# Who makes the fourth pair's x, and which queue stores the last layer's quarters: two lines of a fused attention and two-layer feed-forward kernel

## Chip, cores and metric

The kernel runs on one core of a Trainium2 chip, as one launch. The metric is the device time of an execution in microseconds (us). Three executions of the kernel before gave 876.63, 877.24 and 878.43 us; the median is 877.24.

## What is computed

Four batches of 576 tokens, eight heads of 64, go through an attention with exponential features, and the 2304 resulting tokens of 512 numbers through two feed-forward blocks:

```python
def phi(x):
    proj = np.einsum('bhsd,df->bhsf', x, w_phi)          # 64 -> 128 features
    proj = proj - np.max(np.abs(proj), axis=-1, keepdims=True)
    return np.concatenate([np.exp(proj), np.exp(-proj)], axis=-1)
q_p, k_p = (phi(q), phi(k))
kv = np.einsum('bhsf,bhsd->bhfd', k_p, v)
z = np.sum(k_p, axis=2)
x = np.einsum('bhsf,bhfd->bhsd', q_p, kv) / (np.einsum('bhsf,bhf->bhs', q_p, z)[..., None] + 1e-06)
# x as 2304 x 512
x = np.maximum(np.maximum(x @ w1, x @ w2), x @ w3) @ w_out      # 512 -> 768 -> 512
h = x @ w_in                                                    # 512 -> 2048
g = np.maximum(h, 0.0) + alpha * np.minimum(h, 0.0)
out = g @ w_out2                                                # 2048 -> 512
```

## The kernel before

**Stages.** A *pair* is two heads of one batch; there are 16, four to a batch. For each pair `keys` and `queries` project, take exponentials, and form the numerators and denominators. At the end of `queries` the denominators `nd` are copied to a small tile `dc` by DMA (L388), inverted on VectorE (L390, L391), written to device memory `r_d` (L393), read back broadcast over the 64 rows of each head into `xr` (L400, four DMAs), multiplied with the numerators (L402), and split into a high and a low part `x` (hi: L64 on ScalarE or L405 on GpSimd; lo: L70). Of each pair there are two halves of 288 tokens. With four pairs of a batch done, `layer1` can run: a *unit* is three products `p` of w1, w2, w3 with the x of all four pairs; its result is taken from PSUM by ScalarE (`s`, L436) and VectorE (L437, L439), and stored as `h_d` (L441). Attention of later pairs and units of earlier batches share TensorE for the first 370 us. Then come the product with w_out (L675, in eight *chunks* of 288 tokens, whose results `yo` ScalarE copies out of PSUM at L679), the first product of the second block (L773) and the last one (L861), both in a form with seven products where a plain one has eight.

**Conversions.** All this is done in float32 made of two parts, and the weights come as float64. A list `todo` of steps converts them: a load `st` (L493, from SyncE's queue, three buffers), four operations per tile on ScalarE (L77, L80) and VectorE (L84, L86) that make a word `wt` (eight buffers), and then either a split into the parts that TensorE reads (`wo`, `wi`), or, for the last layer's *quarters*, sums of words (L514) that `park` stores to `q_d` (L527), 28 stores of 256 KB in all. A word's buffer is free when its store has landed. The steps of quarters 0 and 1 and of w_out run at about 320 to 370 us, those of quarters 2 and 3 at 445 to 500 us. The stores are read back from 564 us on.

**What sets the order.** Each engine works through its own list, in order; the list is made when the kernel is built, by a scheduler with its own estimates of durations, from the program's order and from priorities (`tc.high_priority`). So an instruction that waits holds all that stands behind it on its engine, and moving one line can reorder much. SyncE (SP) and GpSimd (POOL) issue DMAs from such lists too. Unlike SP, GpSimd also computes: in the kernel before it makes x for the pairs 0 to 2 (`e = G`), VectorE and ScalarE for all others.

Of the kernel before, what the change touches and what calls it, by code (L numbers as in the profile page):

```python
# [23 lines left out]
NPAIR = H // 2  # L24
# [23 lines left out]
def tile_kernel(ctx: ExitStack, tc: tile.TileContext, qT, kT, tails, v, w_phi, w1, w2, w3, w_out, w_in, w_out2, alpha, out):  # L48
# [11 lines left out]
    nc = tc.nc  # L60
    V, A, G = nc.vector, nc.scalar, nc.gpsimd

    def hi_act(dst, src):
        A.activation(dst, src, AF.Copy)  # L64
# [4 lines left out]
    def sub(eng, dst, src, hi):  # L69
        eng.tensor_tensor(dst, src, hi.bitcast(F32), op=ALU.subtract)  # L70
# [36 lines left out]
    q_d = dram.tile([4, 7, P, 512], F32, name="q_d")  # L107
# [11 lines left out]
    def at(shape, dtype, name, tag=None, bufs=1):  # L119
        pool = ap if (tag or name) in KEYS_ONLY else lp  # L120
        return pool.tile(shape, dtype, name=name, tag=tag or name, bufs=bufs)
# [34 lines left out]
    def i_of(pair):  # L156
        return pair[0] * NPAIR + pair[1]
# [177 lines left out]
    def queries(pair):  # L335
# [26 lines left out]
        for g, tiles, pp in chain(project_queries(pair), tail()):  # L362
# [8 lines left out]
            if plain_kv(pair):  # L371
                e = dst[0]
            else:
                e = at([P, 2, 2, 256], F32, tag="qe", bufs=2, name="qe")[:, :, :, :w]
# [20 lines left out]
        for c in range(2):  # L395
            cs = slice(c * CH, (c + 1) * CH)
            xr = raw_tile()
            for h in range(2):
                r = slice(h * D, (h + 1) * D)
                nc.gpsimd.dma_start(xr[r], rows[h : h + 1, cs].to_broadcast([D, CH]))  # L400
            e = G if i_of(pair) < NPAIR - 1 else V
            e.tensor_tensor(xr, nd[0][:, cs], xr, op=ALU.mult)  # L402
            xh, xl = x_tiles(c)
            if e is G:
                G.tensor_copy(xh, xr)  # L405
            else:
                hi_act(xh, xr)
            sub(e, xl, xr, xh)
            res.append((xh, xl))
        xs[pair[0]].append(res)  # L410

    def raw_tile():
        return xs_.tile([P, CH], F32, tag="xr", bufs=3, name="xr")

    def x_tiles(half):
        t = x_tile(half)
        return t[:, 0], t[:, 1]
# [35 lines left out]
    for i, pair in enumerate(pairs):  # L453
        if i + 1 < len(pairs):
            load_pair(pairs[i + 1])
        with tc.high_priority(offset=(0, SOON, NOW, NOW)[pair[0]]):
            if i == PLAIN - 1:
                hi_dve(wph, wraw)
                sub(V, wpl, wraw, wph)
            run(*([at_priority(LATER, queries(last))] if last else []), keys(pair))  # L460
            last = pair
        count = CONVERT_IN[i] if i < len(CONVERT_IN) else 0
        for j in range(count):
            for _ in range(min(count, 4) if j == 0 else int(j + 3 < count)):
                fetch(begun[pair])
            with tc.high_priority(offset=LAST if i < NPAIR - 1 else 0):
                n = sum(len(x) for x in w)
                run(split_w123(n // 3, n % 3))
        u0 = 3 * (i - NPAIR) - LAG
        for u in range(u0, u0 + 3):  # L470
            if u >= 0:
                c, f = (u % 2, u // 2) if u < 12 else (u // NF1 % 2, u % NF1)
                layer1(u // 12, c, f, xs[u // 12], w[f])
    ap_ctx.close()
    sp = ctx.enter_context(tc.tile_pool(reuse_waits="tile", name="sp", bufs=1, side="right"))
    with tc.high_priority(offset=NOW):
        run(queries(last))
# [46 lines left out]
        return [lambda k=k: split_out(k) for k in range(NF1)], [w_out[k] for k in range(NF1)]  # L524

    def park(p, i, x):
        nc.gpsimd.dma_start(q_d[p, i], x)  # L527

    def do_quarters(p):
        b = {}  # L530

        def get(q):
            b[q] = words()

        def one():
            get(0)
            b[4] = both(word(), b[1], b[0])
            park(p, 0, b[0])
            park(p, 4, b[4])

        def two():
            get(3)
            park(p, 2, b[3])
            b[5] = both(word(), b[3], b[4])
            park(p, 5, b[5])
            park(p, 6, both(b[1], b[3], b[1]))

        def three_():
            get(2)
            park(p, 1, b[2])  # L550
            park(p, 3, both(word(), b[5], b[2]))

        return [lambda: get(1), one, two, three_], [w_out2[p, q] for q in (1, 0, 3, 2)]
# [388 lines left out]
```

## Time and profile before

| | us |
|---|---|
| median of three executions | 877.24 |
| the profiled execution's own time | 878.6 |
| its span, first to last instruction | 876.8 |
| TensorE matmul busy in the span | 868.5 (99%) |
| VectorE / ScalarE / GpSimd busy | 637.3 / 514.5 / 158.4 |

TensorE's granted clock is 1.0, the 2.4 GHz level, in all 40 slices. The busy figure of TensorE counts a matmul until its modelled end; a short wait shows as a gap between starts that is wider than the usual one. So the profile is read here by starts: the rows of TensorE in order of time, then the engine that the late row waits for, then what held that engine.

### The profile page before, as it was taken

What the parts mean: (1) busy time and instruction counts of PE and PEld (TensorE: products, weight loads), DVE (VectorE), ACT (ScalarE), POOL (GpSimd) and SP (SyncE); (2) the same over time, 40 slices, a digit from 0 to 9 for tenths busy, and PEclk for the clock granted to TensorE, in tenths of its full rate; (3) what the DMA queues carried; (4) which work ended last, traced back from release to release, by engine and by line L of the source; (5) the groups of instructions that cost most, each with busy time, mean ns of one, the idle gap of its engine ahead of it and who ended that gap; (6) DMA issues with size and microseconds to landing.
All of it is one profiled execution on the core that took longest, in us unless ns stands there. A gap on an engine that the chain in (4) does not pass through costs nothing.

```text
span 876.8 us, 17441 instructions
## 1 busy us (share of the span) xinstructions
PE 868.5 (99%) x6631; PEld 854.9 (97%) x6631; DVE 637.3 (73%) x1196; ACT 514.5 (59%) x1055; POOL 158.4 (18%) x278
## 2 busy tenths in 40 slices
PE   9999999999999999999999999999999999999998
PEld 8888899999999999999999999999999999999998
DVE  5578878877888776683965754846478899988871
ACT  4666767777677765553853554646477763544440
POOL 0354222112322244211112301111111000000000
PEclk9999999999999999999999999999999999999999
DMA  6445653223332169661688863745348746433321
GB/s 234 140 157 161 180 154 113 76 86 85 88 89 70 36 215 349 212 208 35 195 266 309 314 230 134 225 182 189 123 136 265 268 158 202 150 125 121 120 74 49
DMA packets 70436, 142.99 MB, mean 163 GB/s; under 512 B 9152, under 2 KB 36176, under 8 KB 70352
## 3 DMA queue, kind: packets, MB, share of 16 engines
q1 hardware_dynamic: 53664, 92.95, 33.2%
q0 software_dynamic: 14816, 45.26, 15.0%
q10 hardware_dynamic: 1872, 3.67, 1.2%
q8 instruction: 52, 0.85, 0.4%
q14 instruction: 32, 0.26, 0.1%
HBM read 93.07 MB, written 46.34 MB: 159 GB/s over the span
## 4 chain that ended last, share of the span: by engine, by line
PE 82%; issue 8%; DMA 4%; ACT 3%; DVE 2%; POOL 1%; POOLq 0%; DVEq 0%; ACTq 0%
PE acc L861 20%; PE p L265 16%; PE sums L773 12%; PE pj L265 6%; PE pc L773 6%; PE pn L265 6%; PE kvp L293 4%; PE p L675 3%; PE kvp L306 3%; PE pb L773 3%; DMA st<-in_w_out 2%; PE pt L368 2%; DMA xr<-r_d 1%; DVE wt L86 1%; DMA st<-in_w_in 1%
## 5 line engine op out<-in xcount | busy, mean ns | idle before, releaser
L265 PE MATMUL p<-x,w123t 128*128 128x288 f32 x1728 | 251.4, 298 | 0.4 <-ACT s L436 0.4
L265 PEld LDWEIGHTS p<-x,w123t 128*128 128x128 f32 x1728 | 235.0, 188 | 2.3 <-ACT s L436 0.8
L773 PE MATMUL sums<-x,wi 128*128 128x288 f32 x768 | 107.7, 295 | 0.0
L861 PE MATMUL acc<-wq,o 128*128 128x256 f32 x864 | 105.5, 283 | 0.0
L861 PEld LDWEIGHTS acc<-wq,o 128*128 128x128 f32 x864 | 104.2, 189 | 0.0
L773 PEld LDWEIGHTS sums<-x,wi 128*128 128x128 f32 x768 | 104.0, 188 | 0.0
L861 PE MATMUL acc<-wq,x 128*128 128x256 f32 x648 | 78.1, 280 | 0.0
L675 PE MATMUL p<-x,wo 128*128 128x288 f32 x576 | 77.0, 296 | 0.6 <-ACT yo L679 0.6
L675 PEld LDWEIGHTS p<-x,wo 128*128 128x128 f32 x576 | 76.6, 188 | 0.9 <-ACT yo L679 0.8
L861 PEld LDWEIGHTS acc<-wq,x 128*128 128x128 f32 x648 | 77.0, 188 | 0.0
L792 DVE SCALAR_TENSOR_TENSOR g<-neg,al,g 128x576 f32<-128x576 f32 x64 | 50.3, 811 | 23.6 <-ACT neg L791 23.6
L212 DVE TENSOR_REDUCE mx<-pj 128x4 f32<-128x512 f32 (+1 forms) x80 | 50.1, 628 | 12.3 <-PE pj L265 12.2
L781 ACT ACTIVATE s<-sums 128x576 f32<-128x576 f32 x48 | 31.1, 647 | 42.0 <-PE sums L773 41.9
L77 ACT ACTIVATE wt<-st 128x512 f16<-128x512 bf16 x38 | 30.1, 799 | 42.5 <-DVE wt L514 14.0
L793 POOL DMA_DIRECT2D g_d<-g x32 | 22.9, 715 | 167.2 <-DVE g L792 165.4
L441 POOL DMA_DIRECT2D h_d<-ho x48 | 28.2, 587 | 137.8 <-DVE ho L439 116.3
L245 ACT ACTIVATE ke<-pj,mx 128x128 f32<-128x128 f32 x96 | 36.9, 384 | 14.7 <-DVE mx L212 14.5
L293 PEld LDWEIGHTS kvp<-v,ke 128*128 128x128 f32 x320 | 40.6, 191 | 4.7 <-ACT kvf L318 1.8
L293 PE MATMUL kvp<-v,ke 128*128 128x128 f32 x320 | 42.9, 278 | 1.6 <-ACT kvf L318 1.6
L791 ACT ACTIVATE neg<-g 128x576 f32<-128x576 f32 x64 | 40.2, 675 | 6.3 <-DVE g L823 5.9
L64 ACT ACTIVATE o<-wt 128x512 fp32r<-128x512 f32 x45 | 27.4, 627 | 24.7 <-PE acc L861 14.2
L400 POOL DMA_DIRECT2D xr<-r_d x64 | 34.1, 539 | 32.3 <-DMA r_d<-dc 21.6
(161 smaller groups left out, 1779.6 us busy)
## 6 DMA issues: line engine op xcount, KB each, us to landing
g_d<-g POOLq DMA_DIRECT2D x32, 576.0 KB, 3.6
a<-g_d SPq DMA_DIRECT2D x36, 512.0 KB, 4.3
st<-in_w_out SPq DMA_DIRECT2D x22, 512.0 KB, 5.8
wst<-in_w SPq DMA_DIRECT2D x18, 512.0 KB, 4.0
st<-in_w_in SPq DMA_DIRECT2D x16, 512.0 KB, 4.7
yr<-y_d SPq DMA_DIRECT2D x28, 288.0 KB, 3.9
v<-in_v SPq DMA_DIRECT2D x16, 480.0 KB, 4.4
q_d<-wt POOLq DMA_DIRECT2D x28, 256.0 KB, 5.3
```

Source lines behind the costliest of these rows:

```text
L77: order(A.activation(half[:, :, 1].bitcast(F16), lanes[:, :, 3].bitcast(BF16), AF.Copy))
L212: V.tensor_reduce(mx, pv, axis=AX.X, op=ALU.max, apply_absolute_value=True, negate=True)
L245: A.activation(ev[:, a, 0], pv[:, a], AF.Exp, bias=mx[:, a : a + 1])
L265: nc.tensor.matmul(dst, x, y, start=i == 0, stop=i == len(ops) - 1, **kw)
L293: nc.tensor.matmul(kvp[:, j * P : (j + 1) * P], e[:, c], rv[:, t, j // 2 : j // 2 + 2].rearrange("p a d -> p (a d)"), start=first, stop=t ...
L400: nc.gpsimd.dma_start(xr[r], rows[h : h + 1, cs].to_broadcast([D, CH]))
L675: nc.tensor.matmul(p2[m // 2][1][:, m % 2], x, y, start=k + n == 0, stop=k == NF1 - 1 and n == 2)
L773: nc.tensor.matmul(dst[:, j], a, b, start=start and n == 0, stop=n == len(ops) - 1, skip_group_check=True)
L781: A.activation(s, src, AF.Copy)
L791: A.activation(neg, gv[:, j], AF.Relu, scale=-1.0)
L792: V.scalar_tensor_tensor(gv[:, j], neg, al[:, f + j : f + j + 1], gv[:, j], op0=ALU.mult, op1=ALU.add)
L861: nc.tensor.matmul(acc[i], x, y, start=half == 0 and f == 0 and n == 0 and place[i][1] == 0, stop=half == 1 and f == 3 and n == 2, skip_gr ...
```

## The change

Two lines. `e` in `queries` becomes GpSimd for the pairs 0 to 3 instead of 0 to 2, so for the fourth pair L402, L405 (instead of L64) and L70 are GpSimd's, twice each. And `park` issues its store from SP's queue.

```diff
             for h in range(2):
                 r = slice(h * D, (h + 1) * D)
                 nc.gpsimd.dma_start(xr[r], rows[h : h + 1, cs].to_broadcast([D, CH]))
-            e = G if i_of(pair) < NPAIR - 1 else V
+            e = G if i_of(pair) < NPAIR else V
             e.tensor_tensor(xr, nd[0][:, cs], xr, op=ALU.mult)
             xh, xl = x_tiles(c)
             if e is G:
@@
     def park(p, i, x):
-        nc.gpsimd.dma_start(q_d[p, i], x)
+        nc.sync.dma_start(q_d[p, i], x)
```

The instruction lists differ from the fourth pair on, on every engine. Three places follow.

**At 82 to 92 us.** GpSimd before, from the four loads of the fourth pair's `xr` on:

```order
L400 DMA xr<-r_d 64x288 x4
L388 DMA dc<-nd 64x1x9 x2
L389 DMA nd<-nd 64x576
L441 DMA h_d<-ho 128x288
L393 DMA r_d<-dc 128x9
L400 DMA xr<-r_d 64x288 x4
```

And now, from the same four loads on:

```order
L400 DMA xr<-r_d 64x288 x4
L402 TENSOR_TENSOR xr<-nd,xr 128x288
L388 DMA dc<-nd 64x1x9
L405 CAST x<-xr 128x288
L402 TENSOR_TENSOR xr<-nd,xr 128x288
L70 TENSOR_TENSOR x<-xr,x 128x288
L405 CAST x<-xr 128x288
L388 DMA dc<-nd 64x1x9
L389 DMA nd<-nd 64x576
L70 TENSOR_TENSOR x<-xr,x 128x288
L393 DMA r_d<-dc 128x9
```

Six computing instructions stand between the `xr` loads and the next pair's `r_d` store; the second half's lo part is behind the next pair's `dc` and `nd` DMAs.

TensorE before at that time, from the third product of the first unit that reads the fourth pair's x (`p_803`, `p_816`, `p_829` are its three results):

```order
L265 MATMUL p_829<-x,w123t 128x288
L265 MATMUL p_803<-x,w123t 128x288 x2
L265 MATMUL p_816<-x,w123t 128x288 x2
L265 MATMUL p_829<-x,w123t 128x288 x2
L293 MATMUL kvp<-v,ke 128x128 x7
L265 MATMUL pj<-wph,xhk 128x256
```

And now, from inside the first of the moved groups on:

```order
L265 MATMUL pj<-wpl,xhk 128x256
L265 MATMUL pj<-wph,xlk 128x256
L265 MATMUL pj<-wph,xht 128x256
L265 MATMUL pj<-wpl,xht 128x256
L265 MATMUL pj<-wph,xlt 128x256
L368 MATMUL pt<-ident,pp 128x128 x4
L265 MATMUL p_803<-x,w123t 128x288 x2
L265 MATMUL p_816<-x,w123t 128x288 x2
L265 MATMUL p_829<-x,w123t 128x288 x2
L293 MATMUL kvp<-v,ke 128x128 x8
```

Nine projections `pj` and four transposes `pt`, which stood behind the `kvp` group, now stand between the unit's first three products with the fourth pair's x and its last six.

**At 350 to 374 us.** ScalarE before, from the copy `s_4473` of a unit to `s_4836`:

```order
L436 ACTIVATE s_4473<-p_4434 128x288
L77 ACTIVATE wt<-st 128x512
L80 ACTIVATE st<-st 128x512
L436 ACTIVATE s_4746<-p_4707 128x288
L64 ACTIVATE x<-xr 128x288
L64 ACTIVATE wo<-wt 128x512
L436 ACTIVATE s_4791<-p_4752 128x288
L64 ACTIVATE wo<-wt 128x512 x5
L64 ACTIVATE x<-xr 128x288
L77 ACTIVATE wt<-st 128x512
L80 ACTIVATE st<-st 128x512
L436 ACTIVATE s_4836<-p_4797 128x288
```

And now, from `s_4746` on:

```order
L436 ACTIVATE s_4746<-p_4707 128x288
L77 ACTIVATE wt<-st 128x512
L80 ACTIVATE st<-st 128x512
L77 ACTIVATE wt<-st 128x512
L80 ACTIVATE st<-st 128x512
L64 ACTIVATE x<-xr 128x288
L436 ACTIVATE s_4791<-p_4752 128x288
L64 ACTIVATE wo<-wt 128x512 x6
L77 ACTIVATE wt<-st 128x512
L64 ACTIVATE x<-xr 128x288
L80 ACTIVATE st<-st 128x512
L436 ACTIVATE s_4836<-p_4797 128x288
```

The unit copies keep their order; the conversions L77 and L80 come about one unit later against them, and all six `wo` behind `s_4791`.

**At 466 to 487 us.** ScalarE before, around the copies `yo` of the fourth chunk (`yo<-p_6192` and `yo<-p_6193`):

```order
L77 ACTIVATE wt<-st 128x512
L681 DMA y_d<-yo 128x576
L80 ACTIVATE st<-st 128x512
L64 ACTIVATE x<-hr 128x576 x2
L77 ACTIVATE wt<-st 128x512
L679 ACTIVATE yo<-p_6192 128x576
L80 ACTIVATE st<-st 128x512
L64 ACTIVATE x<-hr 128x576
L679 ACTIVATE yo<-p_6193 128x576
```

And now:

```order
L77 ACTIVATE wt<-st 128x512
L80 ACTIVATE st<-st 128x512
L64 ACTIVATE x<-hr 128x576
L679 ACTIVATE yo<-p_6192 128x576
L64 ACTIVATE x<-hr 128x576
L679 ACTIVATE yo<-p_6193 128x576
L77 ACTIVATE wt<-st 128x512
L683 DMA y_d<-yo 128x576
L80 ACTIVATE st<-st 128x512
```

The second conversion has gone from ahead of both copies to behind both.

## Rows read from the trace of the kernel before

**Rows 1.** The page, busy us of each engine (share of the span) and instructions

```profile
PE 868.5 (99%) x6631; PEld 854.9 (97%) x6631; DVE 637.3 (73%) x1196; ACT 514.5 (59%) x1055; POOL 158.4 (18%) x278
```

**Rows 2.** The chain that ended last, in order of time: start us, us, what

```profile
373.85 34.13 PE p L265 x255
```

**Rows 3.** Timeline of PE from 86 us: start, us, instruction, [idle before <-releaser]

```profile
87.28 1.59 PE L265 MATMUL p<-x,w123t 128*128 128x288 f32 x9
90.45 1.83 PE L293 MATMUL kvp<-v,ke 128*128 128x128 f32 x14 [1.57 <-ACT kvf L318]
```

**Rows 4.** Timeline of ACT, 86 to 91 us

```profile
86.35 0.44 ACT L64 ACTIVATE x<-xr 128x288 fp32r<-128x288 f32 x1 [1.56 <-DVE xr L402]
...
87.91 0.45 ACT L64 ACTIVATE x<-xr 128x288 fp32r<-128x288 f32 x1
...
89.74 0.66 ACT L318 ACTIVATE kvf<-kvp 128x512 f32<-128x512 f32 x1
```

**Rows 5.** Timeline of DVE, 85 to 90 us

```profile
85.86 0.46 DVE L402 TENSOR_TENSOR xr<-nd,xr 128x288 f32<-128x288 f32 x1 [1.73 <-DMA xr<-r_d]
86.23 0.68 DVE L212 TENSOR_REDUCE mx<-pj 128x4 f32<-128x512 f32 x1
...
88.70 0.68 DVE L70 TENSOR_TENSOR xlq<-q,xhq 128x512 fp32r<-128x512 f32 x1
89.30 0.45 DVE L84 TENSOR_SCALAR wt<-wst 128x512 uint16<-128x512 uint16 x1
```

**Rows 6.** Timeline of POOL, 70 to 73 us: GpSimd makes the third pair's x

```profile
70.08 0.43 POOL L405 CAST x<-xr 128x288 fp32r<-128x288 f32 x1
70.47 0.80 POOL L402 TENSOR_TENSOR xr<-nd,xr 128x288 f32<-128x288 f32 x1
71.23 0.80 POOL L70 TENSOR_TENSOR x<-xr,x 128x288 fp32r<-128x288 f32 x1
71.99 0.66 POOL L405 CAST x<-xr 128x288 fp32r<-128x288 f32 x1
```

**Rows 7.** Timeline of DVE beside it

```profile
69.97 2.40 DVE L84 TENSOR_SCALAR wt<-wst 128x512 uint16<-128x512 uint16 x1
```

**Rows 8.** Timeline of PE around 355, 373 and 487 us

```profile
354.33 5.47 PE L265 MATMUL p<-x,w123t 128*128 128x288 f32 x36
...
371.27 2.18 PE L265 MATMUL p<-x,w123t 128*128 128x288 f32 x15
373.85 0.92 PE L265 MATMUL p<-x,w123t 128*128 128x288 f32 x5 [0.40 <-ACT s L436]
...
483.73 2.68 PE L675 MATMUL p<-x,wo 128*128 128x288 f32 x18
487.02 1.20 PE L675 MATMUL p<-x,wo 128*128 128x288 f32 x7 [0.61 <-ACT yo L679]
```

**Rows 9.** Timeline of ACT around 350 to 374 us

```profile
350.45 0.80 ACT L77 ACTIVATE wt<-st 128x512 f16<-128x512 bf16 x1 [3.42 <-DMA h_d<-ho]
...
367.91 0.45 ACT L64 ACTIVATE x<-xr 128x288 fp32r<-128x288 f32 x1 [5.14 <-DVE xr L402]
...
369.07 2.70 ACT L64 ACTIVATE wo<-wt 128x512 fp32r<-128x512 f32 x5
...
373.40 0.40 ACT L436 ACTIVATE s<-p 128x288 f32<-128x288 f32 x1
```

**Rows 10.** Timeline of ACT at 484 us, and of POOL ahead of it

```profile
479.50 0.54 POOL L527 DMA_DIRECT2D q_d<-wt  x1 [0.18 <-issue]
...
484.01 0.80 ACT L77 ACTIVATE wt<-st 128x512 f16<-128x512 bf16 x1 [5.11 <-issue]
...
486.33 0.64 ACT L679 ACTIVATE yo<-p 128x576 f32<-128x576 f32 x1
```

**Rows 11.** Waits: engine, line <- releaser: total us, times, longest; last row q_d's landing

```profile
SPq L603 <- DVE x L70: 33.8, 14, 7.9
...
DMA to landing us min/median/max: 2.7/5.2/7.9
```

## The prediction

> **What bounds the kernel now.** I read the busy line of the page first: TensorE is busy for 868.5 of 876.8 us, VectorE for 637.3, ScalarE for 514.5, GpSimd for 158.4 [rows 1]. So the bound is TensorE, and its clock stays at the upper level throughout. The change leaves the set of matmuls alone. It can move the end only through the places where TensorE's stream has a hole. To find the holes I took the length of a full stream from the chain of waits: 255 products of 128x288 in 34.13 us, 0.134 us each [rows 2]. Then I walked TensorE's timeline by starts, and wherever the next group begins later than count times 0.134 there is a hole.
>
> Up to about 82 us the instruction lists of both kernels are alike, so the start is the same in both. Behind that I find four holes:
>
> - At 87.28 nine products begin. They should end at 87.28 + 9 x 0.134 = 88.49, and the switch to the next kind of matmul costs some 0.2 (my estimate). The next row, `kvp`, begins at 90.45 and waited for ScalarE's `kvf` [rows 3]: a hole of 1.77.
> - At 354.33, 36 products take 5.47 where 4.82 are due [rows 8]. The modelled tail of the last one is some 0.1, so the hole is 0.54.
> - At 371.27, 15 products (2.01) should reach 373.28; the next begins at 373.85, after ScalarE's `s` [rows 8]: 0.57.
> - At 483.73, 18 products (2.41) should reach 486.14; the next begins at 487.02, after ScalarE's `yo` [rows 8]: 0.88.
>
> All four end on ScalarE, so the next view is its timeline. At 86.35 it had waited 1.56 us for VectorE's `xr`, and it then made two casts of x (0.44 and 0.45) in front of the exponentials, so that `kvf` came only at 89.74 [rows 4]. At 350.45 a conversion L77 had waited 3.42, at 367.91 a cast of x had waited 5.14 for `xr`, and behind that five `wo` copies (2.70) stood ahead of `s` at 373.40 [rows 9]. At 484.01 a conversion had waited 5.11 behind a store that GpSimd issued at 479.50, and the second `yo` came at 486.33 [rows 10].
>
> **Part 1: GpSimd makes the fourth pair's x.** Removed are two casts on ScalarE (0.9) and four operations on VectorE (two of L402 at 0.46, two of L70 at 0.45, [rows 5]); six operations on GpSimd are added. ScalarE loses the wait of 1.56 and the casts, so `kvf` comes at some 88.3 to 88.9, before TensorE can get to `kvp`, which now stands behind more work. The hole of 1.77 goes. Two things are late next.
>
> First, x itself. `xr` landed when VectorE began at 85.86 [rows 5]. On GpSimd the multiplication takes 0.80 and the cast 0.43 to 0.66 [rows 6]; between them now stands a DMA to `dc`, at the 0.54 of another issue on GpSimd [rows 10]. That gives 85.86 + 0.80 + 0.54 + 0.43 to 0.66 = 87.6 to 87.9, where TensorE arrives at 87.28 [rows 3]: a hole of 0.35 to 0.58. I take 0.5.
>
> Second, the moved projections. TensorE now does three products, six projections of 256 columns (by columns 0.134 x 256/288 = 0.12 each), and then `pj` with `xht`, which needs the buffer that VectorE's `pp` (L216) empties. It arrives there at about 87.8 + 3 x 0.134 + 6 x 0.12 = 88.9. On VectorE `pp` stands behind the `mx` that ended its wait, `xlq` (0.68) and the conversion L84 (0.45) [rows 5]. With the x work gone, L84 comes up for execution from 87.3 on, just when GpSimd is at the cast. What happens then is in one row: at 69.97, beside the third pair's x on GpSimd, the same L84 took 2.40 instead of 0.45 [rows 7], until after the cast (70.08), the multiplication (70.47) and the subtraction (71.23 to 72.03) [rows 6]. It was held for 2.40 - 0.45 = 1.95. In the changed kernel cast, multiplication and subtraction last from 87.2 to about 89.4. So L84 ends near 89.6, and `pp`, a 128x512 operation like the 0.68 ones [rows 5], at about 90.2. Less 88.9 that is a hole of 1.1 to 1.3. I take 1.1; it is zero if `pp` gets in first.
>
> The sum here is 0.5 + 1.1 - 1.77 = **-0.2**. The ends are -1.5 (x at its early time, `pp` not held) and +0.6 (TensorE waits for the whole x chain, and L84 is held once more for half a microsecond). The lo half of the second x stands behind the next pair's DMAs and is ready near 92, where the products that read it come some microseconds later; I cost it at nothing. If that cover went, it would be one multiplication, 0.80 [rows 6].
>
> Here a rule speaks against the change. The row shows L84 held for 1.95 us, through three operations of GpSimd [rows 6, 7]. The Trainium skill, "SBUF — State Buffer", section "Who interferes with whom", says that VectorE and GpSimd share one pair of ports, that whichever begins first keeps it for its whole instruction, and that the other is blocked meanwhile. The trace agrees that there is blocking, but by that rule L84 would have waited for one GpSimd instruction. I go by the row for the sum; the other reading is a rival below.
>
> **Part 2: the last layer's stores go to SP.** The issue itself (0.54 each, [rows 10]) leaves GpSimd, which is not the bound. What matters is when a store goes out, since a word's buffer is free only when its store has landed, 2.7 to 7.9 us later, 5.2 in the middle [rows 11], and ScalarE's L77 waits for that with unit copies or `yo` queued behind it. Together with the altered order:
>
> - 350 to 374 us. The conversions stand about one unit later against the unit copies, the six `wo` all behind `s_4791`, and the last pairs' inversion L390 and L391 stands some four conversions earlier on VectorE. Each of the two holes is shorter than what it loses from in front of it (0.54 against a wait of 3.42; 0.57 against five `wo` of 2.70, [rows 8, 9]). I take both as gone: **-1.1**. The ends are -1.1 and 0.
> - 485 us. The L77 that had waited until 484.01 now stands behind both `yo`. The second `yo` then starts when its products are done. **-0.9**; the ends are -0.9 and 0.
> - SP works in order. A store there stands behind loads that themselves wait. The nearest rows are SP's waits at L603, 33.8 us in 14 waits, 2.4 in the mean, 7.9 the longest [rows 11]. Most stores come right behind a load `st` that waits for the same VectorE operation, so I take nothing for this; the other end is a rival.
>
> **The sum.** -0.2 - 1.1 - 0.9 = -2.2. Against the profiled execution's 878.6 that gives 876.4. That execution lies 1.4 above the median of 877.24, so on the median the forecast is **875.0**. What this kernel's measurement can tell from no change is about 0.2%, 1.75 us.
>
> **The rivals.**
>
> *The hold on L84 is short.* If L84 is blocked for one GpSimd instruction only, it waits 0.6 for the cast, `pp` ends near 88.9, and TensorE has no second hole there. The first place is then worth 0.5 - 1.77 = -1.3, the whole -3.3: 873.9. For it speaks that a hold depends on which of the two begins first; against it that [rows 7] shows the long one at the same pair of operations. The rule on the shared ports gives this case.
>
> *The holes at 354, 373 and 487 only move.* TensorE's results must be taken by ScalarE, whose work is not less there: the same conversions stand a little later, and the next copy may find them in front of it. Then only the first place remains: -0.2, 877.0. For it speaks that ScalarE waits come from landings of stores [rows 9, 11], which stay as long; against it that L77 and the `yo` have changed places outright.
>
> *Slower: a store stuck on SP.* A store of quarters 2 and 3 stands behind a load L603 whose buffer is not yet free; the word's buffer comes free later, an L77 on ScalarE waits, and a `yo` behind it holds TensorE. The hole at 487 shows that `yo` there has no slack [rows 8]. With a hold between the mean and the longest of SP's waits, (2.4 + 7.9)/2 = 5.2 [rows 11], the time is -2.2 + 5.2 = +3.0: 880.2. It comes out slower than the kernel before from a hold of 2.2, and measurably so from 4.0. Against it: on GpSimd the store stood in a queue that works in order too, and eight words give room.
>
> *The change does nothing.* The lists exclude that: all engines' orders differ at the places named.
>
> **How the numbers follow.** The forecast has a chance of 0.44, of which 0.12 falls short of 1.75 us because a part of one gain is missing; the short hold 0.10; the holes that only move 0.28, of which 0.02 comes out slower by a new hole; the stuck store 0.18, 0.02 of it too small to measure. Faster: 0.32 + 0.10 = 0.42. Same: 0.12 + 0.26 + 0.02 = 0.40. Slower: 0.02 + 0.16 = 0.18. The lower end of the range takes every best end, -1.5 - 1.1 - 0.9 = -3.5, and the 0.6 by which the fastest run lies below the median: 873.1. The upper end takes the first place at +0.6 with no gain elsewhere, 877.8, and the 1.2 by which the slowest run lies above the median: 879.0. Beyond it lies most of the stuck store, some 0.17.
>
> **What would show it.** Right, if after the change `kvp` follows without a wait for `kvf`; TensorE waits about 0.5 for GpSimd's x near 87.3 and about 1.1 for VectorE's `pp` near 89, with an L84 of over 2 us beside GpSimd's cast; there is no hole before the products at 373 and 487; and GpSimd has no rows of L527. An L84 of 0.45 to 1.1 there would show the short hold. New waits of TensorE for `s` or `yo` at neighbouring units would show that holes only moved; a wait on SP ahead of a store, with a long L77 and a late `yo` behind, the stuck store. The forecast is wrong if either shows up with more than half a microsecond, or if a hole opens where none of these places is.

## The result, and the profile after

The changed kernel takes 883.86 us (median of 8 executions, 881.55 to 889.21) against 877.84 for the kernel before (8 executions, 876.09 to 881.20). The ratio is 1.0073, 95% interval 1.0048 to 1.0098: slower by 0.7%, where 875.0 had been forecast, and beyond the upper end of the range, 879.0. The profiled execution has a span of 882.3 us, 5.5 more than that of the kernel before. (One execution of an experiment below, 995.8 us, ran at a mean granted clock of 0.798; it is left out of every comparison, and that kernel was run a second time.)

TensorE's work is the same set of matmuls in both kernels. So the two traces can be laid side by side by count: wherever the first n matmuls, in order of their starts, are the same set in both, the difference between the starts of the next one is what the changed kernel has lost by then. This table is worked out in that way:

| matmuls issued | before, at us | after, at us | after is late by |
|---|---|---|---|
| 362 | 61.20 | 61.48 | 0.28 |
| 578 | 94.64 | 94.75 | 0.11 |
| 661 | 105.91 | 106.37 | 0.46 |
| 808 | 125.69 | 130.54 | 4.85 |
| 2405 | 330.91 | 336.51 | 5.60 |
| 2719 | 373.85 | 380.28 | 6.43 |
| 3560 | 485.59 | 491.68 | 6.09 |
| 3565 | 487.02 | 492.35 | 5.33 |
| last | 873.05 | 878.27 | 5.23 |

In this pair of traces the place at 82 to 92 us gained 0.2, as forecast, and the place at 487 us gained 0.8. At 331 to 374 us, where 1.1 was to be gained, 0.8 was lost, and another 0.8 between 126 and 331 us. But most of the loss, 4.4 us, arose between 106 and 126 us, at a place of which the prediction doesn't speak. (A second trace of the changed kernel, from one of the experiments, loses 4.35 between the same two counts.) TensorE after, in order of time (start, us, instruction, idle before and its releaser; what answers to [rows 3], and the new place):

```profile
87.54 0.80 PE L265 MATMUL p<-x,w123t 128*128 128x288 f32 x3
88.72 0.39 PE L265 MATMUL pj<-wph,xhk 128*128 128x256 f32 x1 [0.38 <-ACT ke L246]
...
90.44 0.36 PE L265 MATMUL pj<-wph,xht 128*128 128x256 f32 x1 [0.76 <-DVE pp L216]
...
116.97 1.01 PE L265 MATMUL p<-x,w123t 128*128 128x288 f32 x5
120.43 0.49 PE L293 MATMUL kvp<-v,ke 128*128 128x128 f32 x2 [2.45 <-ACT ke L245]
120.67 3.05 PE L265 MATMUL p<-x,w123t 128*128 128x288 f32 x12
123.52 0.41 PE L265 MATMUL pj<-wph,xht 128*128 128x256 f32 x1
```

At 120.43 TensorE had stood still for 2.45 us. And the twelve products behind it took 123.52 - 120.67 = 2.85 us, where twelve take 1.61 at the upper level [rows 2]. The granted clock by stretches (window in us, its length, PE busy and count, clock, DMA share, GB/s) tells why:

```profile
119.00:120.00 1.00, 0.00 (x0) 1.00 0.00 0
120.00:121.00 1.00, 0.57 (x4) 0.94 0.00 0
121.00:122.00 1.00, 1.00 (x6) 0.50 0.20 14
...
123.00:124.00 1.00, 1.00 (x7) 0.50 0.87 111
124.00:125.00 1.00, 1.00 (x9) 0.85 0.41 96
```

From about 121 to 124.3 us it is 0.50, the 1.2 GHz level, right behind the time in which TensorE did nothing. That costs half of some 3.4 us: 1.7. Hole and clock together are 4.2 of the 4.4 us.

Who was late is read on the other engines. ScalarE, VectorE and GpSimd after, in this order, each by its timeline:

```profile
110.90 0.45 ACT L357 ACTIVATE nd<-pn 128x320 f32<-128x320 f32 x1
...
120.01 0.37 ACT L245 ACTIVATE ke<-pj,mx 128x128 f32<-128x128 f32 x1 [5.61 <-DVE mx L212]
```

```profile
117.94 0.17 DVE L390 TENSOR_SCALAR dc<-dc 128x9 f32<-128x9 f32 x1 [3.68 <-DMA dc<-nd]
...
118.69 1.28 DVE L212 TENSOR_REDUCE mx<-pj 128x4 f32<-128x512 f32 x2
```

```profile
112.61 0.54 POOL L388 DMA_DIRECT2D dc<-nd  x1 [1.75 <-ACT q L377]
```

Read backwards: `kvp` waits for an exponential `ke` of the eighth pair's keys, that for the maximum `mx`, and `mx` stood on VectorE behind L390, the first step of the inversion of the sixth pair's denominators. L390 waited 3.68 us for the DMA that brings them, which GpSimd had issued at 112.61; and that stood behind the copy `nd` on ScalarE at 110.90. TensorE had finished the projections that `mx` reads by 111.9. The same copy, L390, `mx`, `ke` and `kvp` in the kernel before (rows of its ScalarE, of its VectorE, and of ScalarE and TensorE):

```profile
107.98 0.44 ACT L357 ACTIVATE nd<-pn 128x320 f32<-128x320 f32 x1 [0.61 <-PE pn L265]
```

```profile
114.04 0.17 DVE L390 TENSOR_SCALAR dc<-dc 128x9 f32<-128x9 f32 x1 [3.03 <-DMA dc<-nd]
...
118.68 0.68 DVE L212 TENSOR_REDUCE mx<-pj 128x4 f32<-128x512 f32 x1
```

```profile
119.94 0.37 ACT L245 ACTIVATE ke<-pj,mx 128x128 f32<-128x128 f32 x1
120.64 0.38 PE L293 MATMUL kvp<-v,ke 128*128 128x128 f32 x2
```

Two things differ. The copy is 2.9 us later after the change, since in ScalarE's list it now stands behind seven more exponentials, a cast of a weight and a conversion; L390 gets its data 3.9 us later. And TensorE's list asks for the product earlier: in the kernel before 767 matmuls stand ahead of it, now 740. TensorE arrives at 118.0, where in the kernel before it had other products to do until 120.64. There VectorE waited 3.03 for the same DMA, and no matmul was late for it. The margin was small even so: the exponential `ke` that this `kvp` reads ended at 119.94 + 0.37 = 120.31, 0.33 before the product began.

### The profile page after: what moved, and what is told of

Its sections match the earlier page's. It is cut to its first block, busy times and chain, and to the rows that moved or that the text cites. A ratio compares the mean times of both kernels' runs of the same rounds, so it can differ in the third digit from the quotient of the medians.

```text
span 882.3 us, 17422 instructions
## 1 busy us (share of the span) xinstructions
PE 871.5 (99%) x6631; PEld 857.2 (97%) x6631; DVE 639.6 (72%) x1192; ACT 514.9 (58%) x1053; POOL 147.6 (17%) x256
## 4 chain that ended last, share of the span: by engine, by line
PE 78%; DMA 4%; DVE 2%; issue 1%; ACT 1%; POOL 0%; DVEq 0%; ACTq 0%
PE acc L861 20%; PE p L265 18%; PE sums L773 12%; PE p L675 9%; PE pc L773 6%; PE pn L265 3%; PE kvp L306 3%; PE pj L265 3%; PE pb L773 3%; DMA st<-in_w_out 1%; DMA xr<-r_d 1%; PE pt L368 1%; DMA st<-in_w_in 1%; DMA r_d<-dc 1%; PE kvt L325 0%
## 5 line engine op out<-in xcount | busy, mean ns | idle before, releaser
L77 ACT ACTIVATE wt<-st 128x512 f16<-128x512 bf16 x38 | 30.0, 797 | 39.3 <-DMA st<-in_w_out 11.0
L293 PEld LDWEIGHTS kvp<-v,ke 128*128 128x128 f32 x320 | 40.2, 191 | 5.2 <-ACT ke L245 3.2
L293 PE MATMUL kvp<-v,ke 128*128 128x128 f32 x320 | 42.4, 278 | 2.8 <-ACT ke L245 2.7
L64 ACT ACTIVATE o<-wt 128x512 fp32r<-128x512 f32 x45 | 27.4, 627 | 25.1 <-PE acc L861 13.4
```

The source lines that it names most:

```text
L77: order(A.activation(half[:, :, 1].bitcast(F16), lanes[:, :, 3].bitcast(BF16), AF.Copy))
L293: nc.tensor.matmul(kvp[:, j * P : (j + 1) * P], e[:, c], rv[:, t, j // 2 : j // 2 + 2].rearrange("p a d -> p (a d)"), start=first, stop=t ...
```

## The experiments

Each was compared with the kernel before on the same chip, whose median lay between 877.1 and 878.0. An edit moves the lines behind it, so in the rows of some experiments L390 is L393 or L411, and L293 is L296, L297 or L302.

**One line at a time.** First only x on GpSimd, then only the stores on SP: each is the changed kernel with the other line of the diff as it was before.

> The first line alone: GpSimd makes the fourth pair's x, the stores stay on GpSimd. All engines' lists equal those of the changed kernel up to about 320 us. Theory (the whole loss lies at 104 to 132 us, in the order that the first line brings: a hole of 2.5 us ahead of kvp at 120 us, 1.7 us at the lower clock behind it, and two small holes): the same loss there, so about 6 us above the kernel before, and a granted clock of 0.998 to 0.999 in most runs; behind 320 us the row of the kernel before (0.57 at 373, 0.9 at 487), so 883 to 885. Rival (the stores on SP bring the loss, by filling the DMA engines or by holding ScalarE): 877 or below.

> The second line alone: the stores of the quarters go out from SP, x as in the kernel before. All lists equal those of the kernel before up to about 320 us. Theory: no hole at 120 us, clock 1.000, the 0.9 at 487 us goes, and 355 to 373 us stays within half a microsecond of the kernel before; so 0.4 to 1.4 below it, 876.5 to 877.5. Rival (the stores on SP bring the loss): 4 to 6 above it.

The first line alone gives 885.10 (ratio 1.0095, 1.0081 to 1.0109). Its trace has the hole ahead of `kvp` at 120.60, 2.0 long, and by the count of matmuls it is 4.1 late at 808: the loss is that of the first line. It also has holes at 350 to 362 us that come to 2.4. Whether the stores cost more from GpSimd than from SP in this order can't be told: the intervals of this kernel and of the changed one overlap. The second line alone came out at 878.94 (1.0028, 1.0013 to 1.0043), against the expectation of a gain. It was run again:

> The second line alone, once more, for a profile at the upper clock. The run before gave 879.0 against 877.1, 1.9 above the kernel before, where 0.4 to 1.4 below had been expected. Theory now (the gain of 0.9 at 487 us is there, but at 340 to 380 us new waits come that cost more): holes of 2 to 3.5 us in all at 340 to 380 us, none before, none at 487; 878 to 880. Rival (the difference is noise between runs): 876 to 877.5.

881.33 (1.0039, 1.0022 to 1.0055): slower again, so the second line is no gain either when it stands alone. There is no hole at 487 us; a new one is at 342. TensorE and VectorE of this kernel, and its windows:

```profile
342.40 3.77 PE L265 MATMUL p<-x,w123t 128*128 128x288 f32 x15 [2.19 <-DVE ho L439]
```

```profile
338.65 0.48 DVE L84 TENSOR_SCALAR wt<-st 128x512 uint16<-128x512 uint16 x1 [0.74 <-DMA st<-in_w_out]
340.91 0.46 DVE L402 TENSOR_TENSOR xr<-nd,xr 128x288 f32<-128x288 f32 x1 [1.79 <-DMA xr<-r_d]
...
341.89 0.45 DVE L439 TENSOR_TENSOR ho<-p,s 128x288 f32<-128x288 f32 x1
```

```profile
338.00:340.00 2.00, 2.00 (x17) 1.00 1.05 405
...
341.00:342.00 1.00, 0.00 (x0) 1.00 1.05 402
...
343.00:344.00 1.00, 1.00 (x6) 0.50 1.49 184
```

VectorE waits in its list for the DMA that brings `xr`, and `ho`, which frees TensorE's bank, stands behind that. The same two rows of VectorE in the kernel before:

```profile
337.62 0.44 DVE L439 TENSOR_TENSOR ho<-p,s 128x288 f32<-128x288 f32 x1
...
344.05 0.45 DVE L402 TENSOR_TENSOR xr<-nd,xr 128x288 f32<-128x288 f32 x1
```

There `ho` stands ahead of the multiplication that needs `xr`, and no matmul is late. So this hole is made as the one at 120 us is: a new order has put short work for TensorE behind a wait for a DMA. Again the clock goes to 0.50 behind it. The DMA engines are full (shares of 1.0, 400 GB/s), but they are as full in the kernel before (a share of 1.02, 400 GB/s at 340 to 345 us), and the transfers are only somewhat slower: at 328 to 350 us the median landing is 7.8 us for the stores (6.1 in the kernel before) and 7.1 for `xr` (6.5). How much of the hole that adds was not tried. It is not the hold that the rival in the prediction had: SP's waits at L603 are shorter than before (10.8 us in 10 waits, against [rows 11]).

**Pinning the late copy.** An order edge without a wait puts one row of ScalarE's list ahead of others; the other lists are then made anew too, TensorE's from its 678th matmul on:

```diff
+                pin = i_of(pair) == 7 and g == 0 and a > 0
+                with tc.issue_after(copied[5].ins) if pin else nullcontext():
                     A.activation(ev[:, a, 0], pv[:, a], AF.Exp, bias=mx[:, a : a + 1])
                     A.activation(ev[:, a, 1], pv[:, a], AF.Exp, bias=my[:, a : a + 1], scale=-1.0)
...
-                A.activation(nd[h][:, o : o + w], pn[:, :w], AF.Copy)
+                copied[i_of(pair)] = A.activation(nd[h][:, o : o + w], pn[:, :w], AF.Copy)
```

> The changed kernel, with one thing pinned on ScalarE: the copy of the sixth pair's second half of denominators (nd) stands ahead of six exponentials of the eighth pair's keys, as it does in the kernel before, not behind them. Theory (this copy is 2.9 us late; the inversion of the denominators on VectorE waits 3.7 us for it through a DMA, with the maximum mx and so the exponential behind it that kvp on TensorE waits for): the hole of 2.5 at 120 us and the lower clock behind it go, 4.2 us together, so 879 to 880.5. Rival (kvp is late because VectorE and ScalarE have too much to do there, whatever waits): the hole stays, 883 to 885.

880.41 (1.0036, 1.0023 to 1.0048), the time that the theory gave, with the clock at 1.000 in all five executions. But its trace doesn't show what the theory said. TensorE's waits there:

```profile
108.24 0.49 PE L296 MATMUL kvp<-v,ke 128*128 128x128 f32 x2 [1.64 <-ACT ke L247]
...
122.01 0.49 PE L296 MATMUL kvp<-v,ke 128*128 128x128 f32 x2 [0.32 <-ACT ke L247]
```

```profile
117.89 0.17 DVE L393 TENSOR_SCALAR dc<-dc 128x9 f32<-128x9 f32 x1 [1.40 <-DMA dc<-nd]
```

ScalarE had waited 3.02 us for an `xr` just ahead, and the copy came at 112.76, later than the 110.90 of the changed kernel; L390 ran at 117.89, as there. The hole of 1.64 lies ahead of the point where TensorE's lists differ, behind that late `xr`; the second trace of the changed kernel has one of 1.41 there too. What differs is when the second `kvp` is asked for: 756 matmuls stand ahead of it in place of 740, TensorE comes to it at 121.70 in place of 117.98, and 0.32 of the wait is left. The clock didn't fall. Between 661 and 808 matmuls this kernel loses 1.0 us against the kernel before, where the changed kernel loses 4.4. A further 1.8 was gained at 335 to 377 us, where the lists differ too. So a late L390 does no harm when TensorE asks for `kvp` late enough. That an earlier copy would help isn't shown by this run.

**Moving one product.** The `kvp` product that waits is put behind the next twelve products `p`; nothing else changes in any list:

```diff
+                    pin = i_of(pair) == 7 and t == 2
+                    with tc.issue_after(ready[0, 1, 1, 0].ins) if pin else nullcontext():
                         nc.tensor.matmul(
                             kvp[:, j * P : (j + 1) * P],
...
-            products(p[:, :CH], ops)
+            ready[b, c, f, j] = products(p[:, :CH], ops)
```

> The changed kernel, with a single matmul moved: the kvp product for which TensorE waits at 118 to 120.4 us goes behind the next 12 products p of a unit, which are ready; on the four other engines the lists are unchanged. The wait of VectorE stays. Theory (hole and clock are two costs, and the clock falls because TensorE stood still for 2.4 us): 12 x 0.134 = 1.6 of the hole is filled, a hole of 0.9 remains, and the clock stays at 1.000, which gives back 1.7 more: 3.3 below the changed kernel, 880 to 881.3. Rival (the clock falls for another reason): 1.6 below, 882 to 882.6, with the clock still at 0.998. Rival (the products are not ready either): no gain.

886.33 (1.0109, 1.0095 to 1.0123): no gain, and 2 above the changed kernel's first median. In its trace a pause of 1.84 us stands at 51 us, where its lists are those of the changed kernel and of the kernel before; so it was run once more, with the changed kernel itself beside it.

> The same kernel as in the run with one product moved (886.3), on one chip with the changed kernel itself. In the first run it had a pause of 1.8 us at 51 us, where its lists are those of the changed kernel, and its hole came 12 products later, at 123 to 125 us, 2.0 long, with the clock at the lower level behind it. Theory (the hole only moves to the next product that needs VectorE, so nothing is won; the pause at 51 us is something of this build or of this chip): within 1 of the changed kernel beside it if the pause is of the chip, 2 above it if it is of the build.

> The changed kernel itself, on the same chip as the other three. Theory: 6 above the kernel before, 883 to 885, with a hole of 2 to 2.6 ahead of kvp at 120 us and the clock at 0.998 to 0.999 in most runs, at 1.000 where that hole is shorter. If this chip has a pause at 51 us for this kernel too, 885 to 887.

885.22 (1.0088, 1.0069 to 1.0107) and 884.61 (1.0078, 1.0061 to 1.0096): the same, as far as these intervals tell. The pause at 51 us was in neither trace. TensorE of the kernel with the moved product in this run:

```profile
120.34 0.49 PE L297 MATMUL kvp<-v,ke 128*128 128x128 f32 x2 [1.08 <-ACT ke L245]
...
122.84 0.55 PE L266 MATMUL pj<-wph,xht 128*128 128x256 f32 x1 [2.01 <-DVE my L243]
```

The twelve products fill part of the hole. Then the next product that needs VectorE waits 2.01 us, and the clock is at 0.998 over the span, as in the changed kernel. Here the hole of a late engine wasn't filled by moving one product: it moved to the next thing that was asked of that engine.

**Taking the wait from in front of the maxima.** The changed kernel again; the inversion of the sixth pair is written out later, and its first step queued behind the maximum of the eighth pair's keys:

```diff
+        if i_of(pair) == 5:
+            held.append(scale(pair, nd, dc))
+            return
...
+        with tc.issue_after(least[0].ins) if i_of(pair) == 5 else nullcontext():
             V.tensor_scalar(dc, dc, EPS, None, op0=ALU.add)
...
+            if i_of(pair) == 7 and g == 1:
+                least.append(latest[0])
```

> The changed kernel with one thing pinned on VectorE: the addition to the sixth pair's denominators (dc), which waits 3.7 us for a DMA, stands behind two maxima mx that are ready, not ahead of them; up to there all lists equal those of the changed kernel, but behind it they differ. Theory (the wait in VectorE's list, not a lack of time on it, makes kvp late): the first kvp product goes at once, 12 products p follow, and the next wait is for pp, which still stands behind the DMA, by about 1.1 us at 120 us in place of 2.5; the clock stays at 1.000; 3 below the changed kernel, 880 to 882. Rival (the maxima are late for another reason): the same hole of 2.5 ahead of the first kvp product, 883 to 885.

VectorE and TensorE of this kernel:

```profile
116.46 1.28 DVE L216 TENSOR_REDUCE mx<-pj 128x4 f32<-128x512 f32 x2
119.10 0.17 DVE L411 TENSOR_SCALAR dc<-dc 128x9 f32<-128x9 f32 x1 [1.36 <-DMA dc<-nd]
```

```profile
119.28 0.38 PE L302 MATMUL kvp<-v,ke 128*128 128x128 f32 x2
...
122.18 0.35 PE L274 MATMUL pj<-wph,xht 128*128 128x256 f32 x1 [0.76 <-DVE my L252]
```

At the place the theory holds. With the maxima ahead of the wait, `kvp` goes at once, 0.76 is left further on, and the clock stays at 1.00 throughout that stretch. By the count of matmuls (808) it is 3.2 behind the kernel before, where the changed kernel on the same chip is 6.1 behind; from 661 on it loses 1.1, the changed kernel 4.4. It reaches no lower time for all that: 884.05 (1.0070, 1.0054 to 1.0086). Its lists differ from there on, and between 348 and 381 us it loses some 3 more, 1.3 of it in one hole. The expected 880 to 882 was wrong by that.

**Is it GpSimd?** The next kernel leaves x where it was. It is the kernel before, with ScalarE's `kvf` pinned ahead of the exponentials that delayed it [rows 4]:

```diff
+                pin = i_of(pair) == 6 and g == 0
+                with tc.issue_after(freed[5].ins) if pin else nullcontext():
                     A.activation(ev[:, a, 0], pv[:, a], AF.Exp, bias=mx[:, a : a + 1])
...
-            A.activation(kvf.rearrange("p a b c -> p (a b c)"), kvp, AF.Copy)
+            freed[i_of(pair)] = A.activation(kvf.rearrange("p a b c -> p (a b c)"), kvp, AF.Copy)
```

> The kernel before, with the eight exponentials of the seventh pair's first group of keys pinned behind the copy kvf that frees the kvp bank. Theory (kvp waits 1.77 us at 88.7 us only because kvf stands behind these exponentials): kvf comes 1.3 to 1.7 earlier, that hole falls to 0.3 to 0.5, 1.3 gained there. All lists change behind it, so other holes may come: 875.8 if nothing else changes, and up to 3 above that if a new hole opens, as it did in the changed kernel. Rival (something else holds kvp): the hole stays.

881.48 (1.0048, 1.0027 to 1.0069). TensorE, ScalarE and VectorE:

```profile
88.93 1.74 PE L296 MATMUL kvp<-v,ke 128*128 128x128 f32 x14
...
120.22 0.49 PE L296 MATMUL kvp<-v,ke 128*128 128x128 f32 x2 [3.01 <-ACT ke L247]
```

```profile
110.52 0.46 ACT L360 ACTIVATE nd<-pn 128x320 f32<-128x320 f32 x1
```

```profile
116.80 0.17 DVE L393 TENSOR_SCALAR dc<-dc 128x9 f32<-128x9 f32 x1 [4.15 <-DMA dc<-nd]
...
118.54 1.23 DVE L212 TENSOR_REDUCE mx<-pj 128x4 f32<-128x512 f32 x2
```

The hole of 1.77 at 90 us is gone entirely, and TensorE is 1.6 early at 105 us. Then the same hole comes at the same place, with the same copy late, the same wait on VectorE and the same maxima behind it; only it is 3.01 long. TensorE's list has 752 matmuls ahead of that `kvp`, again fewer than the 767 of the kernel before. So GpSimd's work on x isn't needed to make it. What the two kernels have in common is that `nd` is late, L390 stands before the maxima, and TensorE comes to `kvp` early.

**Three attempts at a better kernel.** First the kernel before, with SP issuing the stores of quarters 2 and 3 alone; then that together with `kvf` pinned; and last `kvf` pinned together with the copy `nd`, ahead of the last four exponentials (`a > 1`).

```diff
-        nc.gpsimd.dma_start(q_d[p, i], x)
+        (nc.sync if p > 1 else nc.gpsimd).dma_start(q_d[p, i], x)
```

> The kernel before, with only the stores of quarters 2 and 3 (445 to 500 us) issued from SP; those of quarters 0 and 1 stay on GpSimd. TensorE's list is unchanged, ScalarE's differs in a few rows behind 440 us. Theory (the stores on SP gain 0.8 to 0.9 at 487 us and lose only at 320 to 350 us, where the DMA engines are full and the fourth batch's xr has to come through them): no hole at 342, the hole of 0.9 at 487 smaller or gone: 0 to 0.9 below the kernel before, clock 1.000. Rival (the order of ScalarE closed the hole at 487 in the changed kernel, not the queue): no difference, the hole stays.

> The two together: kvf first, and the stores of quarters 2 and 3 from SP. TensorE's list equals that of the kernel with kvf first alone; ScalarE's differs behind 440 us. Theory: the two gains are in places that don't touch, so they add: 0 to 0.9 below the kernel with kvf first alone. Rival: the other order behind 440 us opens a hole there, and it is above.

> The kernel with kvf first (881.5, which has no hole at 89 us but the same hole of 3.0 at 120 us as the changed kernel, behind the same late copy nd), with that copy pinned ahead of the last four exponentials of the eighth pair's first group. Theory (one copy, late on ScalarE, makes the hole in both kernels, and the lower clock follows the hole): the hole at 120 falls by 1 to 3, the clock is at 1.000 in most runs, the four exponentials come 1.7 later and may cost up to 1 at 108 us: 877 to 879.5, about the kernel before. Rival (the hole there has another cause in this kernel): it stays, 880.5 to 882.5.

The first gives 878.19 (1.0014, 0.9999 to 1.0029), which can't be told from the kernel before. TensorE's list is unchanged, and the hole at 487 is gone, TensorE running through:

```profile
477.73 14.51 PE L675 MATMUL p<-x,wo 128*128 128x288 f32 x108
```

```profile
481.50 0.81 ACT L77 ACTIVATE wt<-st 128x512 f16<-128x512 bf16 x1 [6.12 <-DMA q_d<-wt]
```

The conversion that held `yo` still stands ahead of it, but starts at 481.50 in place of 484.01 [rows 10]; TensorE was 0.8 early there, so 1.7 of this is the earlier store. So with the stores on SP the hole closes though the conversion keeps its place. The other order closes it too: with the first line alone, stores on GpSimd, TensorE gains the same 0.76 between 3560 and 3565 matmuls as in the changed kernel. The profiled execution, 877.05, was the fastest of its twelve, and the gain of 0.9 is smaller than what its executions differ by. The two others: 884.67 (1.0081, 1.0057 to 1.0105) and 881.69 (1.0041, 1.0022 to 1.0060). In the one the hole at 120 us was 3.3 long, and a second one came at 351. In the other the hole at 120 fell to 1.9 but didn't go (it stands ahead of the projections that need `pp`, with `kvp` behind them), with another of 1.1 at 108: VectorE waited 3.34 us there for the fifth pair's `xr`, and everything came two microseconds later.

```profile
106.01 0.46 DVE L406 TENSOR_TENSOR xr<-nd,xr 128x288 f32<-128x288 f32 x1 [3.34 <-DMA xr<-r_d]
```

The theory in its first form, that one late copy makes the hole, doesn't hold in this run. None of these kernels is faster than the kernel before.

## Why the prediction was wrong, step by step

**The bound and the method** were right: TensorE, and its holes. What failed is the step from the list of holes to the sum of -2.2, where the last matmul came 5.2 later. The prediction went through the four holes of the kernel before, asked what the new order does to each, and took every other place as free. But all engines' lists were rewritten from the fourth pair on, and the waits that the kernel before hides are as long as those that it shows. VectorE's wait of 3.03 for the denominators stood in its trace at 114 us. The forecast never asked what would happen to it if TensorE came 2.6 us earlier, though the two lists show that 27 fewer matmuls stand ahead of that `kvp`. That term is missing from the sum: +4.4 with the clock. The rivals didn't have it either. Each of them was a mechanism at a place already named. Only the prediction's last sign of being wrong, a hole where none of its places is, describes what came.

**Part 1, 82 to 92 us: -0.2 forecast, -0.2 measured** (0.28 late at 362 matmuls, 0.11 at 578). The agreement is luck. From 362 to 578 matmuls the two traces of the changed kernel take 33.27 and 33.28 us, but five traces of experiments whose lists are the same up to there take 33.81 to 34.80. The kernel before takes 33.44, and two experiments with its lists up to there 33.04 and 32.73: the idle time ahead of `kvp` is 1.57 [rows 3] in its trace, and 1.06 and 1.01 in theirs. By the medians of these ten traces the first place costs 0.8 rather than gaining 0.2. The hole that was to go was read from one execution in which it was long. The parts are off as well. GpSimd's x was no hole: `xr` came 0.65 earlier, and the cast was done when TensorE arrived.

```profile
85.21 0.80 POOL L402 TENSOR_TENSOR xr<-nd,xr 128x288 f32<-128x288 f32 x1 [1.10 <-DMA xr<-r_d]
...
86.52 0.54 POOL L405 CAST x<-xr 128x288 fp32r<-128x288 f32 x1
87.03 0.79 POOL L402 TENSOR_TENSOR xr<-nd,xr 128x288 f32<-128x288 f32 x1
87.78 0.79 POOL L70 TENSOR_TENSOR x<-xr,x 128x288 fp32r<-128x288 f32 x1
```

In its place the projections waited 0.38 for a bank that the exponentials free, and then 0.76 for `pp` (1.1 forecast; 1.06 in the second trace of the kernel, 1.17 to 1.35 in the five others, so this term was well sized). The hold on VectorE is there, though it took `xlq` rather than L84:

```profile
87.31 1.82 DVE L70 TENSOR_TENSOR xlq<-q,xhq 128x512 fp32r<-128x512 f32 x1
89.05 0.67 DVE L84 TENSOR_SCALAR wt<-wst 128x512 uint16<-128x512 uint16 x1
```

`xlq` took 1.82 in place of 0.68 [rows 5]: 0.68 before its end is 88.45, and GpSimd's multiplication and subtraction end at 87.82 and 88.57. It was held through both of them, to within 0.12. The Trainium skill, "SBUF — State Buffer", section "Who interferes with whom", says that a VectorE instruction with two inputs in SBUF, as this one is, contends with a GpSimd instruction that reads SBUF, and that the one that began first blocks the other for its whole instruction. That VectorE is held the trace confirms. By that rule `xlq` should have gone at 87.82; it lost to the next GpSimd instruction as well, as L84 did in [rows 7].

**Part 2, 350 to 374 us: -1.1 forecast, +0.8 measured** (5.60 to 6.43). The two holes went, as said. Others came:

```profile
346.20 24.27 PE L265 MATMUL p<-x,w123t 128*128 128x288 f32 x181 [0.33 <-DVE ho L439]
371.10 1.99 PE L265 MATMUL p<-x,w123t 128*128 128x288 f32 x13 [0.63 <-DVE s L437]
373.28 2.00 PE L265 MATMUL p<-x,w123t 128*128 128x288 f32 x13 [0.20 <-DVE ho L439]
```

All of them wait for VectorE. At the first it had waited 0.63 us for `xr`; at the second it had waited 2.71 us, until 368.46, for a load `st`, and then 1.05 for ScalarE's half of that conversion. The rival that the holes only move came nearest here, but it had them move to ScalarE's copies, at no cost. The step that failed is that a wait was taken as gone because the ScalarE instruction behind which it stood had moved. Nor did all four holes end on ScalarE, as the prediction says: of the one at 354, 0.3 us was a wait for VectorE's `s` (L437) and 0.2 one for ScalarE's.

**Part 2, 487 us: -0.9 forecast, -0.8 measured** (6.09 to 5.33). The mechanism held, though the store was another: the one whose landing released the conversion (483.94) was issued at 478.77, and the one of 479.50 that the prediction names landed only at 484.70. TensorE runs through:

```profile
474.83 15.44 PE L675 MATMUL p<-x,wo 128*128 128x288 f32 x115
```

**The slower side** had a chance of 0.18, on a store stuck on SP. The stores on SP alone do cost 0.3 to 0.4%, but through VectorE's order at 340 us, not through a store stuck on SP; in the changed kernel the hole at that place is 0.33, and most of the loss came from the other line.

What stays open: how much of the 6 us in the medians is the clock. The 14 executions of the changed kernel list granted clocks of 0.996 to 1.000, and their times don't follow these alone (881.55 and 882.81 at 1.000, but 886.39 at 1.000 too). And the hole at 107 us was 0.28 in one trace of this kernel and 1.41 in the other, after a wait for `xr` of 4.37. Which landing is late in an execution, and why, was not tried.

## What to carry to other kernels

Where a list per engine is made anew, walk the new lists at every instruction that waits for a transfer, not only where the old trace has a hole: write down what is queued behind each such wait, and how many of the bound engine's instructions stand ahead of the one that will ask for it. A wait that costs nothing today is a price that the next reordering may call in; keep an instruction that waits for a load from standing ahead of short work for the bound engine. Read the length of a hole from more than one execution before putting it into a sum. And price a hole of TensorE above its length: in the traces of this case eight of the nine holes of 1.9 us and longer went with a fall of the clock to 0.50, which costs up to 1.7 more.

## What the hardware showed that was not expected

The granted clock fell to 0.50 for 3.4 us at the holes of 2.45 and 2.26 (changed kernel, at 120 us, in its two traces), 2.19 (stores on SP, at 342) and 3.01 (`kvf` first). It stayed at 1.00 behind those of 1.57 (kernel before, at 90), 1.64 (copy pinned) and 2.0 (first line alone, in its profile), and fell behind one of 1.88 (`kvf` and copy pinned). The length of the hole alone doesn't order these cases.

GpSimd issued the `dc` DMA at 112.61 although the copy that it needs had ended at 111.35: the profile names a later ScalarE instruction, `q` (L377), as the releaser. In the kernel before the copy ended at 108.42 and the issue came at 109.69. That is 1.3 us in both, which no duration of an instruction shows. Behind the copy of the pair's first head it is 0.29 in both traces (106.65 to 106.94, and 104.83 to 105.12).

VectorE's conversion L82 takes 0.43 where GpSimd is idle. In the changed kernel it took 1.45 from 91.14 on, beside a DMA issue of GpSimd (90.94 to 91.47) and its subtraction (91.48 to 92.30): GpSimd's work on x also slows this conversion. The prediction had priced such a hold for L84 alone.
